# Block-sparse attention before a mixture of experts: scores of two batch elements in the two halves of the array's rows, P and V unsplit in f32

## The chip, the cores and the metric

The kernel runs on one core of a Trainium2 chip. The core has five engines that work at once, each on its own stream of instructions: TensorE (PE in the profile; its weight loads are listed as PEld), VectorE (DVE), ScalarE (ACT), GpSimd (POOL) and SyncE (SP), which here only issues transfers. 16 DMA engines move data between memory (DRAM) and the on-chip SBUF; TensorE writes its results to PSUM. A stationary matrix lies in TensorE's array, one partition of it for each row of the contraction, and the other matrix streams past it column by column. The metric is the time of one execution on the device in microseconds (us), lower is better.

## What is computed

Attention of 4 batch elements, 8 heads, 768 positions and 64 columns a head. Keys are seen in blocks of 32: every query block sees blocks 0 and 23, its own block with its two neighbours, and three blocks drawn at random; query blocks 0 and 23 see all. The output, 3072 tokens of 512 values, goes through the best of 8 experts each. Cut to what matters:

```python
scores = (1.0 / np.sqrt(D)) * np.matmul(q, k.transpose(0, 1, 3, 2))
scores = np.where(mask, scores, -1000000000.0)
scores = scores - np.max(scores, axis=-1, keepdims=True)
attn = np.exp(scores)
attn = attn / (np.sum(attn, axis=-1, keepdims=True) + 1e-09)
o = np.matmul(attn, v)
...
e_idx = np.argmax(x @ w_gate, axis=1)
for e in range(E):
    mask = e_idx == e
    h = np.maximum(x[mask] @ w1[e], 0.0)
    ye = h @ w2[e]
    out[mask] = gate_w[mask, None] * eom[mask, e, None] * ye
```

All values are f32, and the choice of the expert hangs on them, so the kernel keeps nearly f32 precision throughout.

## The kernel before

The batch elements go in two pairs (bp = 0, 1). K of a pair lies in SBUF with the 64 columns of the first element (b = 0) on partitions 0 to 63 and those of the second on 64 to 127 (`kn`). A pair has 8 dense units (query blocks 0 and 23: two elements, four groups of two heads) and 44 sparse units (11 pairs of query blocks, two elements, two groups `hg` of four heads): 104 units in all, and as many steps of the program.

A sparse unit makes these stages: **S** (`pS`), eight f32 products of 32 query columns with 256 key columns into one bank of PSUM; a maximum over the keys (`dM`, a reduction at L500 and a product with -1/8 at L501); **P** = exp (`aE`), which scales by 1/8 and subtracts the maximum on the way; **T** (`pT`), four transposes of P into PSUM; the eviction of T as two f16 tiles, 256 P rounded to f16 on ScalarE (`aH`, tile `ph`, L466) and the rest on VectorE (`dL`, tile `pl`, L473); **O** (`pO`), the product with V; a copy of O to SBUF (`aO`, tile `ob`, L537); and `fin`, `fin2`, which add the two parts of O (L446), take the reciprocal of the sum of P and multiply (L451) into the tile `x`. V too is split in f16: each head has 130 columns, 64 of 64 V rounded, a column of ones (which gives the sum of P), 64 of the rest and a zero. `ph` goes against 129 of them, `pl` against 65, so O takes 24 products. In S all 128 partitions of K and of q are used; the tiles `qz` hold the queries of one element, zeros in the other element's rows.

Keys and values come through rings. `kr` (three buffers) has the 12 blocks of K for a pair of query blocks, copied from `kn` by four engines (`gather_k`, `window_k`, `fixed`). V goes to memory (`vscr`) once, and comes back per pair of query blocks: by plain loads into `vc`, and by two indirect gathers on GpSimd's queue (`gather_v`, L423) into one of two `vt` buffers.

When x of 128 tokens is there, ScalarE casts it (`route_h`, L626) into the only `xq` buffer, GpSimd writes the rest beside it (`route_l`, L630), SP stores both to `xscr` in memory in two transfers (`store_x`, L636), a transposing load brings them back (`route_t`), and the routing's products and VectorE's routing operations follow. After the attention the experts run in slots of 128 tokens, eight pieces of weights to each; the weights are split into f16 parts by ScalarE (L891) and VectorE (L898), some by GpSimd.

Every engine issues its instructions in the order in which the program is written (`in_order`). A step of the program runs the stages of several units, each with its lag: with `LAGS = (0, 2, 3)` unit m makes S, the maximum and P in step m, T and its evictions in step m + 2, O in step m + 3, the copy of O in m + 4, `fin` and `fin2` in m + 5 and m + 6. Within a step the order is

```python
run("pT", "pS", "aH")
...
run("aE0", "dL0", "dM", "dL", "pO", "aO", "aE", "fin")
```

and loads, gathers, preparations of V and the routing are hooked to fixed steps: `at(n, f, ...)`. Dense units have `LAGD = (1, 2, 3)`, and each takes two of the four banks of scores. Units stand in the order (bp, query blocks, b, hg). In the first steps the two elements' halves of q, K and V are loaded in turn, all of b = 0 first, and from step 73 on some splits of the first experts' weights stand between the units' instructions (`AHEAD`).

## Time and profile before

| | us |
|---|---|
| three executions | 711.26, 721.58, 721.63 |
| their median | 721.58 |
| span of the profiled execution | 710.4 |

The span is the time from the first to the last instruction in the profile; the time of an execution also has what lies around it. The profiled execution's own time is not known; its span stands 0.9 us under the fastest of the three times and 11.2 us under their median.

The page and the trace's views show busy times by engine, chains of waits, groups of equal instructions and the timeline. In a group's row stand the line, the engine, the operation, result<-operands with their shapes and the count; then the busy time in us and the mean duration of one in ns; then the idle time of the engine just before them and what ended it. Durations of overlapping instructions of an engine cannot be added up; busy time counts an instant once. The page cuts the span into 40 slices, and the traffic of all its DMA engines in each was:

```profile
GB/s 223 286 259 237 236 247 304 259 224 187 156 197 276 292 270 308 192 260 53 4 294 52 154 330 157 76 230 198 227 50 137 221 61 147 211 50 60 61 264 70
```

A slice is 17.8 us. Attention is in slices 1 to 18, and the highest of those has 308 GB/s. The same row for the window from 42.5 to 309 us alone, in slices of 6.7 us, has 350 as its highest, and 331 as the highest of its last ten:

```profile
GB/s 247 221 235 282 200 140 350 217 272 273 346 254 234 241 314 140 289 284 256 66 113 168 210 246 208 155 322 271 259 257 320 268 297 278 281 331 215 196 185 317
```

### The profile page before, as it was taken

The numbers are of one execution on the slowest core, as the hardware profiler recorded it, in microseconds if no ns is written. First come the engines' busy times: TensorE is split into PE (matmuls) and PEld (weight loads), VectorE is DVE, ScalarE is ACT, GpSimd is POOL, SyncE is SP. The second block draws the span as 40 slices with busy tenths as digits, with TensorE's granted clock in tenths as the row PEclk, the third lists the DMA queues.
The fourth block names the chain that finished last, engine by engine and source line by source line (L and its number), as shares of the span: only waits on it lengthen the run. The fifth ranks groups of instructions, "written<-read, shape, count | busy, mean of one in ns | idle before, by whom it ended". The sixth has DMA issues, their size and how long they took to land.

```text
span 710.4 us, 22455 instructions
## 1 busy us (share of the span) xinstructions
PE 586.8 (83%) x8214; PEld 383.1 (54%) x8214; DVE 630.8 (89%) x999; ACT 480.3 (68%) x868; POOL 428.8 (60%) x421
## 2 busy tenths in 40 slices
PE   7878797698999888967587888888888887887886
PEld 5444454455655445546365556655555565555554
DVE  5988887788879889979579999999999999999993
ACT  2866776486688787855377676776676676676671
POOL 5556666475468887666666556556466466466461
PEclk7999999999999999987889999999999999999999
DMA  8987999897779999993082694376724724812282
GB/s 223 286 259 237 236 247 304 259 224 187 156 197 276 292 270 308 192 260 53 4 294 52 154 330 157 76 230 198 227 50 137 221 61 147 211 50 60 61 264 70
DMA packets 99054, 133.53 MB, mean 188 GB/s; under 512 B 62075, under 2 KB 69115, under 8 KB 98684
## 3 DMA queue, kind: packets, MB, share of 16 engines
q1 hardware_dynamic: 87196, 94.40, 51.7%
q0 software_dynamic: 11744, 37.64, 16.2%
q8 instruction: 67, 1.10, 0.7%
q14 instruction: 47, 0.39, 0.2%
HBM read 183.87 MB, written 20.49 MB: 288 GB/s over the span
## 4 chain that ended last, share of the span: by engine, by line
DVE 36%; DMA 22%; PE 19%; issue 13%; POOL 4%; ACT 3%; SPq 2%; POOLq 0%; ACTq 0%; DVEq 0%
DVE kr L898 17%; DMA xscr<-xq 9%; DVE ws L898 7%; PE h L909 4%; DVE hl L922 4%; PE S L494 4%; DMA vt<-vscr,vidx 3%; PE y L932 3%; PE T L459 2%; DMA kn<-in_k_dram 2%; DVE pl L473 2%; DMA out_dram<-yo,tab 2%; POOL table L757 2%; DVE mx L500 1%; DMA wide<-in_v_dram 1%
## 5 line engine op out<-in xcount | busy, mean ns | idle before, releaser
L898 DVE SCALAR_TENSOR_TENSOR kr<-r,kr 128x1024 f16<-128x1024 f32 (+1 forms) x144 | 231.4, 1655 | 9.4 <-ACT kr L891 9.3
L891 ACT ACTIVATE kr<-r 128x1024 f16<-128x1024 f32 (+1 forms) x171 | 167.0, 1031 | 11.8 <-DMA r<-in_wcat_dram 9.7
L909 PEld LDWEIGHTS <-kr 128*128 128x128 f16 x2004 | 128.6, 99 | 72.2 <-DVE kr L898 33.3
L909 PE MATMUL h<-qz,kr 128*128 128x128 f16 x1884 | 136.8, 220 | 30.5 <-DVE kr L898 28.4
L941 POOL DMA_INDIRECT out_dram<-yo,tab x28 | 30.0, 1073 | 127.3 <-ACT yo L938 121.4
L898 DVE SCALAR_TENSOR_TENSOR ws<-r,ws 128x1024 f16<-128x1024 f32 (+1 forms) x60 | 102.8, 1761 | 0.0
L932 PE MATMUL y<-kr,hh 128*128 128x512 f16 x334 | 100.3, 382 | 0.0
L506 ACT ACTIVATE P<-S,mx 128x256 f32<-128x256 f32 x176 | 75.1, 486 | 36.4 <-DVE mx L501 33.6
L494 PE MATMUL S<-kr,qz 128*32 128x256 f32 x1408 | 96.6, 393 | 0.0
L896 POOL TENSOR_TENSOR kr<-wf,kr 128x1024 f16<-128x1024 f32 x27 | 72.2, 2674 | 21.8 <-issue 10.7
L473 DVE SCALAR_TENSOR_TENSOR pl<-T,ph 128x512 f16<-128x512 f32 x88 | 60.2, 685 | 17.4 <-ACT ph L466 16.3
L500 DVE TENSOR_REDUCE mx<-S 128x2 f32<-128x512 f32 x88 | 59.5, 676 | 13.5 <-PE S L494 13.4
L932 PE MATMUL y<-kr,hl 128*128 128x512 f16 x167 | 64.0, 383 | 3.1 <-DVE hl L922 3.1
L917 ACT ACTIVATE hh<-h 128x512 f16<-128x512 f32 x56 | 33.2, 592 | 46.1 <-PE h L909 46.1
L909 PEld LDWEIGHTS <-ws 128*128 128x128 f16 x684 | 44.0, 100 | 32.4 <-DVE ws L898 18.6
L891 ACT ACTIVATE ws<-r 128x1024 f16<-128x1024 f32 (+1 forms) x60 | 58.0, 1012 | 2.1 <-PE y L932 2.1
L459 PE MATMUL T<-ident,P 128*128 128x128 f32 x352 | 59.1, 292 | 0.3 <-DVE pl0d L473 0.3
L909 PE MATMUL h<-qz,ws 128*128 128x128 f16 x612 | 45.4, 219 | 16.3 <-DVE ws L898 15.6
L466 ACT ACTIVATE ph<-T 128x512 f16<-128x512 f32 x88 | 54.1, 615 | 5.4 <-PE T L459 5.4
L853 POOL DMA_INDIRECT qz<-xscr,tab x28 | 47.9, 1710 | 11.9 <-DMA tab<-table 7.4
L938 ACT ACTIVATE yo<-y,tab 128x512 f32<-128x512 f32 x28 | 19.2, 687 | 52.9 <-PE y L932 52.9
L494 PEld LDWEIGHTS S<-kr,qz 128*32 128x32 f32 x1408 | 37.3, 110 | 31.2 <-issue 14.8
(233 smaller groups left out, 1178.3 us busy)
## 6 DMA issues: line engine op xcount, KB each, us to landing
r<-in_wcat_dram SPq DMA_DIRECT2D x240, 512.0 KB
qz<-in_q_dram SPq DMA_DIRECT2D x48, 128.0 KB
xscr<-xq SPq DMA_DIRECT2D x48, 128.0 KB
vc<-vscr SPq DMA_DIRECT2D x22, 260.0 KB
vscr<-vn SPq DMA_DIRECT2D x12, 260.0 KB
vscr<-vn SPq DMA_DIRECT2D x6, 520.0 KB
kn<-in_k_dram SPq DMA_DIRECT2D x4, 768.0 KB
vs<-in_v_dram SPq DMA_DIRECT2D x6, 512.0 KB
```

The source lines that it names most:

```text
L459: nc.tensor.transpose(pt[:, 128 * c:128 * c + 128], p[:, 128 * c:128 * c + 128], ident)
L466: nc.scalar.activation(ph[:, 0:w], pt[:, 0:w], AF.Copy, scale=SP_)
L473: nc.vector.scalar_tensor_tensor(pl[:, 0:w], pt[:, 0:w], SP_, self.ph[n][:, 0:w], op0=ALU.mult, op1=ALU.subtract)
L494: nc.tensor.matmul(s[64 * h2 + 32 * qi:64 * h2 + 32 * qi + 32, hp], t[:, 64 * j + 32 * qi:64 * j + 32 * qi + 32], g[:, 1 - qi:3:1 + qi, :, ...
L500: nc.vector.tensor_reduce(mx, self.s, axis=AX.X, op=ALU.max)
L506: nc.scalar.activation(p[:, 256 * hp:256 * hp + 256], self.s[:, hp], AF.Exp, bias=self.mx[:, hp:hp + 1], scale=EXPS)
L853: nc.gpsimd.indirect_dma_start(xgs[s], None, src, bass.IndirectOffsetOnAxis(ap=tabs[s][:, 1:2], axis=0))
L891: nc.scalar.activation(w[:, 0, r], piece(n // 8, n % 8)[:, r], AF.Copy, scale=SW)
L896: nc.gpsimd.tensor_tensor(w[:, 1], ws.pop(("f", n)), w[:, 0], op=ALU.subtract)
L898: nc.vector.scalar_tensor_tensor(w[:, 1, r], piece(n // 8, n % 8)[:, r], SW, w[:, 0, r], op0=ALU.mult, op1=ALU.subtract)
L909: nc.tensor.matmul(hps[n // 4][:, 128 * j:128 * j + 128], w[:, hl, 128 * c:128 * c + 128], x[:, c // 2, xl, c % 2], start=cnt == 0, stop=c ...
L932: nc.tensor.matmul(ys[s], a[:, m], w[:, l, 512:1024], start=n % 8 == 0 and cnt == 0, stop=n % 8 == 7 and cnt == 2)
```

## The change

Three things are done, and the order of the work follows them.

**Scores of both elements together.** `qz` is one tile per pair of query blocks with the queries of b = 0 on partitions 0 to 63 and those of b = 1 on 64 to 127; the zeros are gone. The units stand in the order (query blocks, hg, b), so that the two elements' units are neighbours, and the first of the two issues the products of both, in turn on the rows 0 to 63 and 64 to 127, into a bank of each:

```diff
         def pS(self):
+            if self.mate is None:
+                return
             bp, i, b, hg = self.k
-            t, r = qt[bp, i][b], kr[i % RK]
-            s = self.s = psS.tile([128, 2, 256], F32, tag="S", name="S" + self.name)
+            t, r = qt[bp, i], kr[i % RK]
+            both = self, self.mate
+            for u in both:
+                u.s = psS.tile([128, 2, 256], F32, tag="S", name="S" + u.name)
...
                     for qi in range(2):
-                        nc.tensor.matmul(
-                            s[64 * h2 + 32 * qi:64 * h2 + 32 * qi + 32, hp], t[:, 64 * j + 32 * qi:64 * j + 32 * qi + 32],
-                            g[:, 1 - qi:3:1 + qi, :, 32 * j:32 * j + 32], start=True, stop=True)
+                        for b, u in enumerate(both):
+                            p = slice(64 * b, 64 * b + 64)
+                            nc.tensor.matmul(
+                                u.s[64 * h2 + 32 * qi:64 * h2 + 32 * qi + 32, hp],
+                                t[p, 64 * j + 32 * qi:64 * j + 32 * qi + 32],
+                                g[p, 1 - qi:3:1 + qi, :, 32 * j:32 * j + 32], start=True, stop=True)
```

Dense units do the same, so a pair of them takes all four banks of scores at once; `LAGD` becomes (0, 2, 3). At the start q, K and then V are loaded for both elements at once:

```diff
-    load_q(0, NPAIR, (0,))
-    load_k(0, slice(0, 12), slice(0, 64))
-    load_k(0, slice(12, 24), slice(0, 64))
-    for c in range(6):
-        load_v(0, c, (0,), spare(c))
-    load_q(0, NPAIR, (1,))
-    load_k(0, slice(0, 12), slice(64, 128))
-    load_k(0, slice(12, 24), slice(64, 128))
+    load_q(0, NPAIR)
+    load_k(0, slice(0, 12))
+    load_k(0, slice(12, 24))
     for c in range(6):
-        load_v(0, c, (1,), spare(c))
+        load_v(0, c, spare(c))
```

**P and V unsplit.** A head of V has 65 f32 columns (64 and the ones) in place of 130 f16 ones, which is the same number of bytes. V's preparation is one copy per block of 128 keys (`v_in`): for the first pair on GpSimd (four) and VectorE (two), for the second all on GpSimd, where ScalarE rounded and VectorE or GpSimd subtracted before. T is evicted once, as f32, by ScalarE for units of b = 0 and by VectorE for units of b = 1 (in dense units: by ScalarE for the first half of the keys, by VectorE for the second). O takes 12 products; its copy has 65 columns a head where it had 129; the sum of the two parts (L446) is gone.

```diff
+        def evict(self, n, engine):
+            pt, w = self.t[n]
+            p = att.tile([128, 512], F32, tag="pt", name=f"pt{n}" + self.name, bufs=4)
+            if engine == "act":
+                nc.scalar.copy(p[:, 0:w], pt[:, 0:w])
+            else:
+                nc.vector.tensor_copy(p[:, 0:w], pt[:, 0:w])
+            self.pt[n] = p
...
             for hp in range(2):
-                for w, n in ((ph, 129), (pl, 65)):
-                    for h2 in range(2):
-                        col = 256 * hp + 128 + 64 * h2
+                for h2 in range(2):
+                    col = 256 * hp + 128 + 64 * h2
+                    nc.tensor.matmul(
+                        o[64 * h2:64 * h2 + 64, hp, 0:VW], w[:, col:col + 64],
+                        cv[:, b, 4 * h2 + 2 * hg + hp], start=hp == 0, stop=False)
+            for hp in range(2):
+                for h2 in range(2):
+                    for qi in range(2):
+                        col = 256 * hp + 64 * h2 + 32 * qi
                         nc.tensor.matmul(
-                            o[64 * h2:64 * h2 + 64, hp, 0:n], w[:, col:col + 64],
-                            cv[:, b, 4 * h2 + 2 * hg + hp, 0:n], start=hp == 0 and n == 129, stop=False)
...
+                            o[64 * h2 + 32 * qi:64 * h2 + 32 * qi + 32, hp, 0:VW], w[:, col:col + 32],
+                            av[:, qi, b, 4 * h2 + 2 * hg + hp], start=False, stop=hp == 1)
```

**Scale and sign.** The factor 1/8 goes into the copies of K (`eighth` in place of `one`; `fixed`, a copy on GpSimd for the first pair and three loads of 256 KB for the second, becomes two products on GpSimd each time), and a sparse unit's reduction gives the negated maximum by itself:

```diff
-            nc.vector.tensor_reduce(mx, self.s, axis=AX.X, op=ALU.max)
-            nc.vector.tensor_single_scalar(mx, mx, -EXPS, op=ALU.mult)
+            nc.vector.tensor_reduce(mx, self.s, axis=AX.X, op=ALU.max, negate=True)
```

Dense units keep their scale and sign. The experts' input buffers take three new tiles in the place of three of the six old `qz`, and `hh` and `hl` become the halves of a `pt` tile.

How the order of the engines' instructions moves is seen at the second pair's fourth pair of query blocks, on two engines. First TensorE before, from one unit's T over the start and end of the next O to the following T and S. A name has the unit's numbers (bp, i, b, hg; where there are only three, bp is left out), and the last number counts tiles; the shape is that of the result.

```order
L459 MATMUL T_1_3_0_0_5935<-ident,P_3_0_0_5829 128x128 x4
L494 MATMUL S_3_1_0_5940<-kr_182,qz_1_190 32x256 x8
L520 LDWEIGHTS ph_1_2_1_1_5866
L520 MATMUL O_2_1_1_5956<-vc_185,ph_1_2_1_1_5866 64x129
...
L528 MATMUL O_2_1_1_5956<-vt_2_5350,ph_1_2_1_1_5866 32x129
L459 MATMUL T_1_3_0_1_6006<-ident,P_3_0_1_5899 128x128 x4
L494 MATMUL S_3_1_1_6011<-kr_182,qz_1_190 32x256 x8
```

TensorE after, at the same place, from the last scores of one pair of units to the first of the next:

```order
L489 MATMUL S_3_0_0_4621<-kr_180,qz_186 32x256
L489 MATMUL S_3_1_0_4622<-kr_180,qz_186 32x256
L514 MATMUL O_2_1_0_4645<-vc_183,pt_1_2_1_0_4562 64x65 x4
L521 MATMUL O_2_1_0_4645<-vt_2_4274,pt_1_2_1_0_4562 32x65 x8
L440 MATMUL T_1_2_1_1_4684<-ident,P_2_1_1_4578 128x128 x4
L514 MATMUL O_2_0_1_4693<-vc_183,pt_1_2_0_1_4639 64x65 x4
L521 MATMUL O_2_0_1_4693<-vt_2_4274,pt_1_2_0_1_4639 32x65 x8
L440 MATMUL T_1_3_0_0_4743<-ident,P_3_0_0_4660 128x128 x4
L489 MATMUL S_3_0_1_4748<-kr_180,qz_186 32x256
L489 MATMUL S_3_1_1_4749<-kr_180,qz_186 32x256
```

Before, eight products of S stood between every T and the next O; now 16 of two units stand behind every second T, and behind the other T comes O at once.

VectorE before, at two units of the second pair (mx is the maximum, pl the rest of P, den the sum of P, ws a piece of the experts' weights):

```order
L500 TENSOR_REDUCE mx_3_1_0_5951<-S_3_1_0_5940 128x2
L501 TENSOR_SCALAR mx_3_1_0_5951<-mx_3_1_0_5951 128x2
L473 SCALAR_TENSOR_TENSOR pl_1_3_0_0_5954<-T_1_3_0_0_5935,ph_1_3_0_0_5949 128x512
L445 TENSOR_SCALAR den_2_0_1_5986<-ob_2_0_0_5827 128x4
L898 SCALAR_TENSOR_TENSOR ws_5929<-r_5353,ws_5929 128x512
L500 TENSOR_REDUCE mx_3_1_1_6022<-S_3_1_1_6011 128x2
L501 TENSOR_SCALAR mx_3_1_1_6022<-mx_3_1_1_6022 128x2
L473 SCALAR_TENSOR_TENSOR pl_1_3_0_1_6025<-T_1_3_0_1_6006,ph_1_3_0_1_6020 128x512
```

and after, at the same place:

```order
L496 TENSOR_REDUCE mx_3_0_1_4768<-S_3_0_1_4748 128x2
L896 SCALAR_TENSOR_TENSOR ws_4738<-r_4277,ws_4738 128x512
L496 TENSOR_REDUCE mx_3_1_1_4809<-S_3_1_1_4749 128x2
L449 COPY pt_1_3_1_0_4811<-T_1_3_1_0_4804 128x512
L425 TENSOR_SCALAR den_2_0_1_4830<-ob_2_0_0_4658 128x4
L426 RECIPROCAL den_2_0_1_4830<-den_2_0_1_4830 128x4
```

A reduction per unit is left, with a copy for every second one, and the split of weights now stands between the reductions of the two units of a pair. On SP the first loads of K go from four half loads, with V's between them, to two whole ones ahead of all of V.

More of the change, by code (lines that the diff above doesn't have):

```diff
@@ L63 @@
 XE = 102, 104
[L65 removed]
+VH = 17, 21, 26, 33, 37, 42
 XTB = 2
@@ L108, in tile_kernel @@
     psO = actx.enter_context(tc.tile_pool(name="psO", bufs=2, space=PSUM))
-    vscr = [dram.tile([769, 2 * 8 * VW], F16, name=f"vscr{i}") for i in range(2)]
+    vscr = [dram.tile([769, 2 * 8 * VW], F32, name=f"vscr{i}") for i in range(2)]
     xscr = dram.tile([NTOK, 2 * DM], F16, name="xscr")
@@ L322, in tile_kernel @@
     kr = [ring.tile([128, 12, 256], F32, name=f"kr{i}") for i in range(RK)]
-    vc = [ring.tile([128, 2, 8, VW], F16, name=f"vc{i}") for i in range(RV)]
-    qz = [[ring.tile([128, 512], F32, name=f"qz{n}_{b}") for b in range(2)] for n in range(RQ)]
+    vc = [ring.tile([128, 2, 8, VW], F32, name=f"vc{i}") for i in range(RV)]
+    qz = [ring.tile([128, 512], F32, name=f"qz{n}") for n in range(RQ)]
     kn, vn = {}, {}
@@ L367, in store_v, with v_in @@
+        nc.sync.dma_start(buf.rearrange("p (b j w) -> p b j w", b=2, j=8), v[bp, 128 * c:128 * c + 128])
+    def v_in(bp, c, kind):
+        vb = vn[bp][:, c].rearrange("p b j w -> p (b j) w")[:, :, 0:D]
+        vs = ld["v", bp, c].rearrange("p (n w) -> p n w", w=D)
+        if kind == "act":
+            nc.scalar.copy(vb, vs)
+        elif kind == "dve":
+            nc.vector.tensor_copy(vb, vs)
+        else:
+            nc.gpsimd.tensor_copy(vb, vs)
+    def store_v(bp, c):
         nc.sync.dma_start(
-            vscr[bp][128 * c:128 * c + 128, w * bs[0]:w * bs[-1] + w],
@@ L589, in pO @@
             for c in range(6):
-                ph, pl = self.ph[c // 3], self.pl[c // 3]
+                w = self.pt[c // 3]
                 col = 128 * (c % 3)
-                order = ((ph, 129), (pl, 65)) if c < 5 else ((pl, 65), (ph, 129))
-                for w, n in order:
-                    for h2 in range(2):
-                        j = 4 * h2 + u
-                        nc.tensor.matmul(
-                            o[64 * h2:64 * h2 + 64, 0, 0:n], w[:, col + 64 * h2:col + 64 * h2 + 64],
-                            vn[bp][:, c, b, j, 0:n], start=c == 0 and n == 129, stop=c == 5 and n == 129)
+                for h2 in range(2):
+                    nc.tensor.matmul(
+                        o[64 * h2:64 * h2 + 64, 0, 0:VW], w[:, col + 64 * h2:col + 64 * h2 + 64],
+                        vn[bp][:, c, b, 4 * h2 + u], start=c == 0, stop=c == 5)
         def aO(self):
@@ L845, in load_w @@
         nc.sync.dma_start(piece(s, j), src, cond=chg)
-    xbuf = [t for ts in qz for t in ts]
+    xbuf = qz + [ring.tile([128, 512], F32, name=f"xb{i}") for i in range(3)]
     def load_x(s):
@@ L948, in tile_kernel @@
     for bp in range(2):
-        for b in range(2):
-            for u in range(4):
+        for u in range(4):
+            for b in range(2):
                 units.append(Dense(bp, b, u))
         for i in range(NPAIR):
-            for b in range(2):
-                for hg in range(2):
+            for hg in range(2):
+                for b in range(2):
                     units.append(Sparse(bp, i, b, hg))
+    for m in range(0, len(units), 2):
+        units[m].mate = units[m + 1]
     prep_alloc(0)
@@ L996, in tile_kernel @@
     at(12, setup_index)
-    for b in range(2):
-        for c, (n, pool, early) in enumerate(VPREP[b]):
-            at(n, v_hi, 0, c, (b,), early)
-            at(n, v_lo, 0, c, (b,), pool, early)
-            at(n, store_v, 0, c, (b,))
+    for c, (n, kind) in enumerate(VPREP):
+        at(n, v_in, 0, c, kind)
+        at(n, store_v, 0, c)
     at(13, setup_rest)
```

177 lines of the change are left out of this document (72 added, 105 removed).

## The prediction

> **What bounds the kernel now.** First the busy shares, then the span by stage, then the chain of waits inside each attention stage.
>
> ```profile
> PE 586.8 (83%) x8214; PEld 383.1 (54%) x8214; DVE 630.8 (89%) x999; ACT 480.3 (68%) x868; POOL 428.8 (60%) x421
> ```
>
> The shares average over unlike stages. The windows view has one row each for the start with the first pair's dense units, its 44 sparse units, the second pair's dense units, its first 16 and last 28 sparse units, the tail of attention and routing, and the experts.
>
> ```profile
> core 0: us, PE busy (x) PEld busy (x) DVE busy (x) ACT busy (x) POOL busy (x), PEclk, DMA share, GB/s
> 0.00:42.50 42.50, 31.84 (x294) 19.68 (x294) 32.49 (x92) 21.58 (x48) 23.91 (x59) 0.88 0.92 259
> 42.50:168.60 126.10, 105.29 (x2020) 62.06 (x2019) 102.36 (x260) 86.50 (x221) 81.59 (x111) 0.96 0.92 253
> 168.60:195.50 26.90, 24.63 (x339) 14.96 (x336) 22.74 (x76) 18.11 (x47) 13.53 (x18) 0.94 0.61 134
> 195.50:234.30 38.80, 36.94 (x745) 22.17 (x744) 33.69 (x90) 31.24 (x83) 29.05 (x38) 1.00 0.89 241
> 234.30:309.00 74.70, 63.64 (x1281) 37.77 (x1280) 67.49 (x169) 57.42 (x148) 56.48 (x74) 1.00 1.06 269
> 309.00:357.00 48.00, 28.45 (x379) 22.37 (x380) 34.12 (x82) 21.99 (x38) 30.06 (x20) 0.75 0.39 76
> 357.00:710.40 353.40, 296.06 (x3169) 204.13 (x3169) 337.93 (x235) 243.50 (x288) 194.16 (x106) 0.99 0.52 152
> ```
>
> The experts hold half the span with VectorE busy 338 of 353 us, and the change leaves their arithmetic alone: it can only let them start earlier. A sparse unit takes 126.1 / 44 = 2.87, 38.8 / 16 = 2.43 and 74.7 / 28 = 2.67 us in the three sparse stages. TensorE is busy 95% of the middle one, but only 83% and 85% of the others, where the DMA share is 0.92 and 1.06. The chains of those three stages, in order, name what ends last:
>
> ```profile
> by line: DMA xscr<-xq 24.8%; DMA vt<-vscr,vidx 17.9%; PE S L494 11.8%; PE T L459 7.2%; issue 5.2%; PE O L528 3.7%; DVE mx L500 3.6%; DVE pl L473 3.5%; PE O L520 3.4%; SPq L636 2.4%; DVE mx L501 1.5%; DVE den L445 1.3%; ACT ob L537 1.2%; DVE
> by line: PE S L494 20.8%; PE T L459 10.4%; DVE pl L473 9.4%; DVE mx L500 9.4%; DVE mx L501 5.3%; PE Od L596 5.0%; PE O L520 4.1%; PE O L528 3.8%; ACT P L506 3.3%; ACT ph L466 2.8%; issue 2.7%; DVE g L697 2.3%; DVE kr L412 1.7%; PE T1d L459
> by line: DMA xscr<-xq 42.9%; issue 8.6%; PE S L494 4.6%; SPq L636 4.4%; DVE pl L473 3.4%; PE T L459 3.3%; POOL xg L853 2.6%; DVE mx L500 2.5%; SPq L376 2.5%; SPq L642 2.4%; DVE mx L501 2.2%; ACT ph L466 2.1%; ACT ob L537 2.0%; PE O L520 1.9
> ```
>
> So only the middle stage is paced by the engines that the change relieves. The other two wait on two loops of transfers: stores of x (xscr<-xq) from the one xq buffer, and the gather of V (vt) in two buffers. The timeline shows a turn of the first: a cast into xq, two stores, and the next cast, released by the landing.
>
> ```profile
> 259.48 0.62 ACT L626 CAST xq<-x 128x512 f16<-128x512 f32 x1 [1.46 <-DMA xscr<-xq]
> ...
> 262.70 1.37 SPq L636 DMA_DIRECT2D xscr<-xq  x2
> ...
> 270.96 0.62 ACT L626 CAST xq<-x 128x512 f16<-128x512 f32 x1 [2.09 <-DMA xscr<-xq]
> ```
>
> A turn is 270.96 - 259.48 = 11.5 us for four units: 2.87 each, whatever TensorE does, unless the stores land sooner.
>
> **TensorE per unit.** One steady unit on its timeline (start, duration, instruction, count):
>
> ```profile
> 207.44 1.07 PE L494 MATMUL S<-kr,qz 128*32 128x256 f32 x16
> 208.44 0.25 PE L520 MATMUL O<-vc,ph 128*64 128x129 f16 x2
> 208.52 0.20 PE L520 MATMUL O<-vc,pl 128*64 128x65 f16 x2
> ...
> 208.87 0.23 PE L528 MATMUL O<-vt,ph 128*32 128x129 f16 x4
> 209.03 0.66 PE L459 MATMUL T<-ident,P 128*128 128x128 f32 x4
> 209.61 0.42 PE L494 MATMUL S<-kr,qz 128*32 128x256 f32 x4
> ```
>
> S takes 208.44 - 207.44 = 1.00, O 0.59, T 0.58: together 2.17.
>
> - Scores. Eight f32 products stand as 16 rows in four column strips, four deep: 0.25 us for 256 columns, 0.98 ns a column and row. The change puts 16 products for two units there, half of them on rows 0-63 and half on 64-127. If the halves run at once, the pair costs 1.00, or 0.50 a unit; if they take turns, 1.00 a unit. No row here shows two row halves at once. I take overlap, since the column strips do overlap, and keep 1.00 as the other end.
> - P times V. Eight f16 products of 64 columns and 16 of 32 become four and eight in f32, each two rows of 65 columns. Per strip: 2 + 2 products, two rows each, 8 x 65 x 0.98 = 0.51 us streaming. Before, the strip streamed 4 x (129 + 65) = 776 columns; the f16 price follows from products of 512 and 128 columns,
>
> ```profile
> L932 PE MATMUL y<-kr,hh 128*128 128x512 f16 x334 | 100.3, 382 | 0.0
> L909 PE MATMUL h<-qz,kr 128*128 128x128 f16 x1884 | 136.8, 220 | 30.5 <-DVE kr L898 28.4
> ```
>
>  (382 - 220) / 384 = 0.42 ns a column, 0.33 us; so 0.59 - 0.33 = 0.26 was gaps. With all or half of these O becomes 0.77 or 0.64: I take 0.70 (ends 0.51 and 0.90).
> - T is unchanged. New unit: 0.50 + 0.70 + 0.58 = 1.78, a saving of 0.39 (18%).
>
> **The other engines per unit.** ScalarE, VectorE and GpSimd:
>
> ```profile
> L466 ACT ACTIVATE ph<-T 128x512 f16<-128x512 f32 x88 | 54.1, 615 | 5.4 <-PE T L459 5.4
> L473 DVE SCALAR_TENSOR_TENSOR pl<-T,ph 128x512 f16<-128x512 f32 x88 | 60.2, 685 | 17.4 <-ACT ph L466 16.3
> L500 DVE TENSOR_REDUCE mx<-S 128x2 f32<-128x512 f32 x88 | 59.5, 676 | 13.5 <-PE S L494 13.4
> L501 DVE TENSOR_SCALAR mx<-mx 128x2 f32<-128x2 f32 x88 | 29.9, 339 | 3.0
> L446 POOL TENSOR_TENSOR ob<-ob 128x256 f32<-128x256 f32 x41 | 26.7, 650 | 0.0
> L405 POOL TENSOR_TENSOR kr<-kn,one 128x256 f32<-128x256 f32 x66 | 46.0, 697 | 3.7 <-DVE mxd L574 3.2
> L382 POOL COPY kr<-kn 128x512 f32<-128x512 f32 x3 | 1.9, 626 | 0.0
> ```
>
> Each T was evicted twice (615 on ScalarE, then 685 on VectorE); now once, in turn. ScalarE loses 0.31 a unit. VectorE loses 0.685 + 0.339 (the negation goes into the reduction, which stays at 676) and gains half an f32 copy, at 685 at most 0.34: net -0.68. In the middle stage ScalarE was busy 31.24 / 16 = 1.95 a unit and VectorE 2.11; they go to 1.64 and 1.43, under TensorE's 1.78. The exp without a scale and K's copies with one keep their durations: zero, as the copies already multiply (L405 by one). GpSimd loses 27 us of sums of hi and lo. It gains six copies of V (1024 columns; twice the 512-column copy's 626 is 1.25 each, 7.5 in all) and 12 - 3 fixed copies of K at 697, less than 7: about 15, in stages where it is 65% busy. A gather of vt queued behind one of them starts up to 1.25 later; the other end, nothing. The eviction's halves bring one new wait: odd units' O now waits on VectorE alone, behind the expert weights' splits there; before, every O did, through pl. Loads: one 128-partition q instead of two halves takes an issue per pair off SP's queue; V's store and gather move the same bytes (65 f32 for 130 f16).
>
> **Sum by stage.**
> - Start. Its end is tied to V's way to the gather, and first scores wait for K:
>
> ```profile
> 3.15 9.76 DMA wide<-in_v_dram
> 12.92 13.17 DMA kn<-in_k_dram
> 32.42 4.72 DMA vscr<-vn
> 43.98 8.78 DMA vt<-vscr,vidx
> 8.62 1.08 PE L564 MATMUL S0d<-kn,qz 64*64 64x384 f32 x4 [2.71 <-DMA kn<-in_k_dram]
> ```
>
>  Two rounds of half loads end in K at 26.1 and V's store at 32.4. Now K comes whole, then V; q, K and V are 6.6 MB, 25 us at the row's 259 GB/s, and one copy and store follow: about 28 instead of 32. I take -5; ends -9, and +3 if first scores wait for all of K's first half and the dense units run late.
> - Sparse, first pair. If TensorE paced it: 44 x 0.39 = -17. By the chain's shares: PE S, T and O hold 26% of 126 us, of which 18% is 5.9; the negation 1.9; half of pl 2.2: -10. I take -13. Ends: 0 if the loops hold, and -22 if the same bytes moved at the best slice of the page, 308 GB/s, in place of 253.
> - Dense, second pair. A dense pair now takes all four score banks at once, so the next pair's scores wait for the exps: fewer products, a new wait. -2 (-5 to +2).
> - Next 16 units: TensorE-paced, 16 x 0.39 = -6 (0 to -8).
> - Last 28 units: PE shares 10% of 75 us by 18%, negation 1.6, half of pl 1.3: -4; TensorE-paced would be -11. I take -6; ends 0, and -14 at the best slice again (269 to 331).
> - Tail and experts: 0 (5 either way); they start earlier.
>
> Sum: -5 - 13 - 2 - 6 - 6 = -32. The profiled execution's span is 710.4, 0.9 under the fastest run and 11.2 under the median 721.6; its new span would be 678.4. Against the median: 721.6 - 32 = 689.6.
>
> A rule against the full gain: the Trainium skill, TensorEngine Tiling (Array Packing), section "PSUM Bottleneck", says that tiling speeds up TensorE and not the emptying of PSUM, which may then bound. By it the dense pair, whose four banks wait for reductions and exps, would gain 0 rather than 2, and the sum would be -30. The same page, "Key Properties", says that different tiles run matmuls in parallel; by it scores cost 0.50 a unit. No run yet shows either for row halves.
>
> **Rivals.**
> - Loops shrink too. Fewer stalls let SP issue the stores sooner, and the two loops follow TensorE: -5 - 22 - 2 - 8 - 14 = -51, about 671. For: steps pace the issue of the stores. Against: the DMA share is already 0.92 and 1.06. Chance 0.14.
> - Loops hold all. Only start, dense and the middle stage gain: -5 - 2 - 6 = -13, 708.6. For: the 42.9% of the last chain. Against: PE, pl and mx stand on the chains too. Chance 0.18.
> - Row halves take turns. Scores of a pair take 2.00, so a unit is 1.00 + 0.70 + 0.58 = 2.28, 0.11 over now; 88 x 0.11 = +10 gives 731, and with O at 0.90, +27 gives 749. It decides from 1.78 a pair on. For: no row of overlap. Against: the strips overlap. Chance 0.07.
> - The forecast (676 to 707): 0.58. Unnamed slowdowns: 0.03. A lower granted clock is in these: the tail's row has 0.75 at 59% busy, but the first pair's stage would be 88 / 113 = 78% busy, near its 83% with 0.96.
>
> **Numbers.** 2% is 14.4 us (707.2 to 736), about what a measurement of this kernel can tell from no change. Faster: 0.58 + 0.14 + 0.02 of the second rival = 0.74; slower 0.06 (the third with its worse O, and unnamed); same 0.20. The range runs from 662, below the first rival for a longer bound of its 51, to 710, past the second: some 0.2 is left out, mostly above.
>
> **What would show it.** Right: scores of a pair in 1.0 us; O near 0.7; about 1.8 to 2.0 a unit on TensorE in the middle stage; xscr<-xq still heading the last stage's chain with a turn near 11 us; the first sparse scores near 37; experts still 353 us. Wrong: a pair's scores at 2 us; stores landing in 5 us; the dense stage over 29 us; or the experts' stage longer, as its own splits would then hold what attention gave.

## The result and the profile after

| | before | after |
|---|---|---|
| executions (us) | 711.26, 715.08, 721.58, 721.63 | 683.72, 692.33, 692.40, 693.10 |
| median | 718.33 | 692.37 |
| span of the profiled execution | 710.4 | 691.3 |

The changed kernel takes 0.9634 of the time before, 95% interval 0.9534 to 0.9735: faster, by 26 us between the medians. The forecast was 689.6, in a range of 662 to 710. Some executions take over 1.5% longer than the fastest of their kernel; the ratios here and below leave them out, the medians do not. The profiled execution of the changed kernel was its slowest (693.10 for a span of 691.3); that of the kernel before, whose time is not known, has a span 0.9 us under its fastest time. The spans therefore differ by 19 only.

The windows view of the changed kernel, cut at the same places of the program (start, first pair's sparse units, second pair's dense units, its first 16 and last 28 sparse units, tail, experts):

```profile
core 0: us, PE busy (x) PEld busy (x) DVE busy (x) ACT busy (x) POOL busy (x), PEclk, DMA share, GB/s
0.00:35.00 35.00, 26.82 (x296) 17.70 (x296) 20.57 (x79) 12.26 (x28) 16.93 (x51) 0.85 0.90 331
35.00:146.50 111.50, 93.82 (x2020) 61.21 (x2019) 73.01 (x183) 67.52 (x188) 72.88 (x95) 0.97 0.98 281
146.50:174.70 28.20, 23.58 (x335) 15.68 (x333) 21.30 (x65) 14.08 (x37) 13.52 (x18) 0.88 0.58 116
174.70:212.40 37.70, 33.95 (x747) 22.89 (x746) 27.31 (x67) 26.64 (x76) 26.99 (x33) 1.00 0.81 228
212.40:290.50 78.10, 63.92 (x1260) 40.74 (x1263) 46.55 (x127) 48.13 (x133) 50.10 (x60) 0.89 1.00 259
290.50:338.00 47.50, 28.58 (x414) 21.93 (x405) 31.75 (x77) 21.01 (x37) 29.30 (x18) 0.82 0.38 81
338.00:691.30 353.30, 295.33 (x3165) 202.97 (x3163) 337.53 (x235) 243.83 (x288) 195.49 (x106) 0.99 0.52 152
```

By stage the change gave -7.5, -14.6, +1.3, -1.1, +3.4, -0.5 and -0.1 us: 19.1 less in all. Each is the difference of two single executions. How far a stage moves from one execution to the next is seen in two runs below that leave the first pair's sparse stage as it was: it takes 119.1 us in before_start, where the kernel before has 126.1, and 108.0 in after_pre, where the changed kernel has 111.5. VectorE's busy time in the three sparse stages fell from 204 to 147 us and ScalarE's from 175 to 142, and still the last 28 units did not get shorter. What the reader is to see is the last column but one: the DMA engines are busy 0.98 and 1.00 of the two long stages. (The share adds up the times of packets, so it can pass 1, as the 1.06 before did.) The chains of the three sparse stages, in order (issue is time for which the profile shows no wait; SPq and POOLq are the sequencers of SP and GpSimd):

```profile
by line: DMA xscr<-xq 41.6%; issue 14.1%; DMA xT<-xscr 6.1%; PE S L489 4.9%; POOL x L430 4.5%; POOL kr L385 4.2%; POOLq L376 3.6%; PE T L440 2.8%; SPq L634 2.3%; POOL vn L349 1.9%; PE O L514 1.4%; PE O L521 1.3%; POOL vt L403 1.3%; SPq L640
by line: DMA vt<-vscr,vidx 25.8%; DMA xscr<-xq 22.2%; PE T L440 13.8%; PE S L489 12.6%; PE Od L594 6.8%; PE O L521 6.1%; PE O L514 5.1%; issue 4.4%; POOL xq L628 3.1%; POOL vt L403 1.9%; ACT xq L624 1.7%; POOL x L430 1.5%; PE T0d L440 1.3%;
by line: DMA xscr<-xq 47.3%; issue 14.3%; DMA tab<-table 10.5%; DMA table<-vals,place 7.0%; POOL x L430 4.6%; SPq L640 4.3%; POOL vt L403 4.3%; POOL kr L385 2.6%; SPq L634 2.5%; POOL xg L851 2.5%; SPq L822 2.3%; POOL xq L628 2.3%; POOLq L37
```

Transfers now end last in the middle stage too, where TensorE did before. TensorE itself did become quicker. Its timeline at a pair's scores, and at a sparse unit:

```profile
179.10 1.09 PE L489 MATMUL S<-kr,qz 64*32 64x256 f32 x32
180.12 0.57 PE L594 MATMUL Od<-vn,pt0d 128*64 128x65 f32 x12
...
201.31 0.64 PE L440 MATMUL T<-ident,P 128*128 128x128 f32 x4
201.88 0.45 PE L514 MATMUL O<-vc,pt 128*64 128x65 f32 x8
202.26 0.44 PE L521 MATMUL O<-vt,pt 128*32 128x65 f32 x16
202.63 0.66 PE L440 MATMUL T<-ident,P 128*128 128x128 f32 x4
```

The 16 products of two units (32 records, two for each product) take 180.12 - 179.10 = 1.02 us, where the eight of one took 1.00: the row halves run at once. O takes 202.63 - 201.88 = 0.75. With T at 0.58 a unit costs 0.51 + 0.75 + 0.58 = 1.84, against 2.17 before. The groups of the other engines:

```profile
L496 DVE TENSOR_REDUCE mx<-S 128x2 f32<-128x512 f32 x88 | 59.7, 682 | 44.1 <-PE S L489 34.0 <-PE O L514 10.0
L449 DVE COPY pt<-T 128x512 f32<-128x512 f32 x44 | 29.9, 680 | 5.7 <-PE T L440 2.2 <-remote 1.7 <-PE O L521 1.7
L349 POOL COPY vn<-vs 128x1024 f32<-128x1024 f32 x6 | 6.7, 1113 | 0.0
L447 ACT COPY pt<-T 128x512 f32<-128x512 f32 x44 | 25.8, 587 | 30.6 <-PE T L440 25.6 <-remote 3.5 <-PE S L489 1.3
```

The negated reduction stays at its price (682 against 676 ns), the f32 eviction costs VectorE 680 and ScalarE 587, and V's copies 1.11 us each. VectorE's reductions now wait 44 us for TensorE, where they waited 13.5.

### The profile page after: what moved, and what is told of

It is laid out like the page before. It is cut to its first block, busy times and chain, and to the rows that moved or that the text cites. A ratio compares the mean times of both kernels' runs of the same rounds, so it can differ in the third digit from the quotient of the medians.

```text
span 691.3 us, 22003 instructions
## 1 busy us (share of the span) xinstructions
PE 566.0 (82%) x8214; PEld 383.1 (55%) x8214; DVE 558.0 (81%) x829; ACT 433.5 (63%) x784; POOL 405.2 (59%) x379
## 4 chain that ended last, share of the span: by engine, by line
DVE 34%; DMA 23%; issue 16%; PE 14%; POOL 7%; SPq 2%; ACT 2%; POOLq 1%; another core or an unknown queue 0%; DVEq 0%; ACTq 0%
DVE kr L896 19%; DMA xscr<-xq 12%; DVE ws L896 7%; DVE hh L923 4%; PE h L907 3%; PE y L933 2%; POOL table L755 2%; DMA kn<-in_k_dram 2%; DMA tab<-table 2%; DMA out_dram<-yo,tab 2%; PE S L489 1%; DMA vt<-vscr,vidx 1%; POOL x L430 1%; DMA r<-in_wcat_dram 1%; PE T L440 1%
## 5 line engine op out<-in xcount | busy, mean ns | idle before, releaser
L889 ACT ACTIVATE kr<-r 128x1024 f16<-128x1024 f32 (+1 forms) x171 | 167.0, 1031 | 11.6 <-DMA r<-in_wcat_dram 9.5
L933 PE MATMUL y<-kr,hh 128*128 128x512 f16 x501 | 138.3, 381 | 3.3 <-DVE hh L923 2.9
L907 PE MATMUL h<-xb,kr 128*128 128x128 f16 x1344 | 98.1, 220 | 22.5 <-DVE kr L896 21.3
L933 PEld LDWEIGHTS <-hh 128*128 128x128 f16 x672 | 57.1, 99 | 42.8 <-DVE hh L923 15.0
L628 POOL TENSOR_TENSOR xq<-x,xq 128x512 f16<-128x512 f32 x24 | 29.2, 1216 | 62.9 <-ACT xq L624 60.9
L489 PE MATMUL S<-kr,qz 64*32 64x256 f32 x1408 | 62.2, 405 | 3.8 <-issue 3.1
L918 ACT ACTIVATE hh<-h 128x512 f16<-128x512 f32 x56 | 33.2, 592 | 47.5 <-PE h L907 46.6
L440 PE MATMUL T<-ident,P 128*128 128x128 f32 x352 | 59.5, 293 | 0.0
L403 POOL DMA_INDIRECT vt<-vscr,vidx x44 | 44.8, 1018 | 24.6 <-PE O L521 11.2
L521 PE MATMUL O<-vt,pt 128*32 128x65 f32 x1408 | 44.1, 233 | 15.1 <-DMA vt<-vscr,vidx 12.2
L885 POOL TENSOR_TENSOR wf<-r,sw 128x1024 f32<-128x1024 f32 x27 | 52.6, 1947 | 4.5 <-DMA r<-in_wcat_dram 3.9
L514 PE MATMUL O<-vc,pt 128*64 128x65 f32 x704 | 42.2, 239 | 15.7 <-ACT ob L530 11.6
L514 PEld LDWEIGHTS O<-vc,pt 128*64 128x64 f32 x704 | 29.3, 141 | 44.6 <-ACT ob L530 21.2
```

Source lines behind the costliest of these rows:

```text
L403: nc.gpsimd.indirect_dma_start(t[:, s].rearrange("p b j w -> p (b j w)"), None, vscr[bp], bass.IndirectOffsetOnAxis(ap=vidx[:, i, s:s + 1] ...
L440: nc.tensor.transpose(pt[:, 128 * c:128 * c + 128], p[:, 128 * c:128 * c + 128], ident)
L489: nc.tensor.matmul(u.s[64 * h2 + 32 * qi:64 * h2 + 32 * qi + 32, hp], t[p, 64 * j + 32 * qi:64 * j + 32 * qi + 32], g[p, 1 - qi:3:1 + qi, ...
L514: nc.tensor.matmul(o[64 * h2:64 * h2 + 64, hp, 0:VW], w[:, col:col + 64], cv[:, b, 4 * h2 + 2 * hg + hp], start=hp == 0, stop=False)
L885: nc.gpsimd.tensor_tensor(wf, piece(n // 8, n % 8), sw128.to_broadcast([128, 1024]), op=ALU.mult)
L889: nc.scalar.activation(w[:, 0, r], piece(n // 8, n % 8)[:, r], AF.Copy, scale=SW)
```

## The experiments

Each was compared with the kernel before on its own chip; the ratio is of times, with its 95% interval. For the changed kernel itself it is 0.963 (0.953 to 0.974). The profiles of after_xq2, after_pre and after_neg have spans 10, 10 and 9 us above the medians of their times, so a stage that is longer there proves nothing. A difference between two ratios, of runs on different chips, is given with both intervals taken together (as independent).

| run | median us | before us | ratio |
|---|---|---|---|
| after_xq2 | 697.3 | 717.9 | 0.974 (0.967 to 0.981) |
| after_own | 759.7 | 717.9 | 1.062 (1.053 to 1.071) |
| after_block, one time | 699.4 | 717.9 | |
| before_pair | 736.2 | 717.9 | 1.027 (1.018 to 1.035) |
| after_turn | 681.2 | 720.5 | 0.952 (0.942 to 0.962) |
| after_zero | 704.6 | 720.5 | 0.981 (0.972 to 0.989) |
| after_pre | 680.1 | 720.5 | 0.949 (0.941 to 0.957) |
| after_turn_pre | 678.9 | 713.2 | 0.957 (0.947 to 0.967) |
| after_turn_pre_xq2 | 676.4 | 713.2 | 0.950 (0.934 to 0.966) |
| after_neg | 692.1 | 713.2 | 0.974 (0.963 to 0.985) |
| before_start | 712.1 | 713.2 | 1.002 (0.996 to 1.008) |
| zero_turn_pre_xq2 | 709.8 | 718.6 | 0.989 (0.980 to 0.997) |

### Is it the one xq buffer?

```diff
-            xq = rt.tile([128, 2, 2, 256], F16, tag="xq", name=f"xq{tt}", bufs=1)
+            xq = rt.tile([128, 2, 2, 256], F16, tag="xq", name=f"xq{tt}", bufs=2)
```

> The changed kernel with two xq buffers in place of one, nothing else. Theory A (one xq buffer holds the two long sparse stages: a cast waits for the landing of the stores before it, and ScalarE's and GpSimd's queues stand behind it): no cast waits for a landing any more, the last 28 units go from 78 us to 62-68, the first pair's 44 from 111.5 to 97-104, total 18 to 28 us under the changed kernel. Rival B (the transfers' bandwidth is the bound, the wait only shows it): the stages shrink by less than 3 us each, total within 5 us of the changed kernel. Rival C (the gather of vt in its two buffers takes over): half of A, 8 to 14 us.

Not faster: the ratio is 1.0% above the changed kernel's, give or take 1.2. A and C are excluded. B fits, at the edge of its 5 us (697.3 against 692.4): neither long stage shrank, with 117.3 and 81.4 us in a profile 10 us above the median. The waits of the first pair's sparse stage (who waits for whom: us in total, times, longest):

```profile
ACT pt L447 <- PE T L440: 22.8, 10, 6.2
...
PEld O L521 <- DMA vt<-vscr,vidx: 8.5, 3, 5.5
PEld L664 <- DMA xT<-xscr: 8.1, 4, 2.7
...
PE lp L664 <- DMA xT<-xscr: 7.4, 4, 2.6
```

No cast waits for a landing any more. In its place TensorE waits, with its whole queue, for the transposing load of x (the product lp) and for the gather of vt, and ScalarE waits for TensorE. The wait moved one station down the same trip; the buffer did not hold the stage. In the last 28 units the landing of the stores still has 39.8% of the chain (47.3% with one buffer), with the transposing load behind it at 12.2%.

### Do the row halves overlap, and what does pairing give?

The first run takes the mate away, the second only changes the order of a pair's products:

```diff
-            if self.mate is None:
-                return
...
-            both = self, self.mate
+            both = (self,)
...
```

> The changed kernel, but every unit issues its own eight scores' products (on its 64 rows) in its own step: no two row halves at once. If row halves overlap in the changed kernel, S of a unit costs 1.0 us here and 0.64 there. Theory A (TensorE paces only the 16 units in the middle): those 16 units are 4 to 6 us longer, the other sparse stages within 4 us, the dense stage of the second pair 1 to 2 us shorter since no four banks are taken at once; total 2 to 9 us over the changed kernel. Rival (TensorE paces all sparse stages): 0.36 x 88 = 30 us over it.

```diff
-            for hp in range(2):
-                for h2 in range(2):
-                    j = 4 * h2 + 2 * hg + hp
-                    for qi in range(2):
-                        for b, u in enumerate(both):
+            for b, u in enumerate(both):
+                for hp in range(2):
+                    for h2 in range(2):
+                        j = 4 * h2 + 2 * hg + hp
+                        for qi in range(2):
```

> The changed kernel with the 16 products of a sparse pair in another order: eight of the first row half, then eight of the second, in place of taking turns. If the halves run at once only when neighbours in the queue lie on different halves, S of a pair takes 2.0 us in place of 1.28; if TensorE looks further ahead than eight products, it stays at 1.28. If the halves never ran at once in the changed kernel, nothing changes.

In after_block the timeline has a pair's scores at full clock and the O behind them:

```profile
190.61 1.13 PE L489 MATMUL S<-kr,qz 64*32 64x256 f32 x32
191.67 0.45 PE L514 MATMUL O<-vc,pt 128*64 128x65 f32 x8
```

191.67 - 190.61 = 1.06 us: the halves still run at once when eight products of one half stand in the queue ahead of the other's. (The 1.28 in the expectations was the first pair of the changed kernel's middle stage, at 174.72 us; the next took 1.02, and the granted clock was 1.00 at both. Why the first took longer is not shown.) In after_own a unit's scores take 1.0 us, as expected, but the total is 67 us over the changed kernel, more than either theory. The page's row of the granted clock in after_own, by slices of 18.9 us:

```profile
PEclk9999555555559999998888999999999999999999
```

and the window of its low stretch, in the windows view:

```profile
83.30:200.80 117.50, 117.50 (x1303) 64.51 (x1302) 44.02 (x116) 43.65 (x118) 44.25 (x56) 0.50 0.66 173
```

For 117 us TensorE was busy without a pause at half its clock. The clock fell in a stall, of 5.0 us up to 80.8 us, and came back at 229 us, 150 us later, in the second pair's dense units. All four executions have a low mean clock (0.86 to 0.88; the changed kernel's have 0.95 to 0.96), so it is no chance of one profile. So a second experiment gave every unit its own scores with all 128 rows in use, the other element's being zeros, as in the kernel before. It is the unsplit P and V without the pairing:

```diff
-            t, r = qt[bp, i], kr[i % RK]
+            t, r = qt[bp, i][b], kr[i % RK]
...
-                            p = slice(64 * b, 64 * b + 64)
+                            p = slice(0, 128)
...
```

> The changed kernel, but every unit issues its own eight scores' products on all 128 rows, with zeros in the other element's rows (as the kernel before): P and V unsplit alone, with scale, sign and start of the changed kernel. TensorE's unit is 1.0 + 0.75 + 0.59 = 2.33 us, as in the run with 64 rows and no pairs (759.7). Theory K (with products on 64 of the 128 rows only, the granted clock stays at a half once it fell; with all rows in use it comes back within some 7 us): no stretch of 0.5 over 15 us in the sparse stages, first pair's sparse stage 108-120 in place of 163 us, total 695 to 712. Rival (the stretch at half clock came from TensorE having no idle time, whatever the rows): about 755.

Theory K held: 704.6, 55 us under after_own with the same products per unit. Its windows of the first pair's sparse stage and of the last 28 units:

```profile
37.10:163.90 126.80, 112.41 (x2022) 68.81 (x2021) 71.27 (x178) 67.36 (x188) 69.18 (x88) 0.93 0.95 248
228.30:307.80 79.50, 67.61 (x1275) 41.01 (x1276) 51.63 (x125) 47.54 (x133) 49.49 (x58) 1.00 1.06 255
```

The clock is back at 0.93 and 1.00: it fell in stalls here too (of 4.8 us up to 126.8 us, for one), and was at 1.00 again 7 to 10 us after it fell. The first stage is 127 us, over the 108 to 120 expected. Against the kernel before, unsplit P and V with their scale, sign and start give 1.9%; pairing then gives the rest, 704.6 to 692.4 (1.7%, give or take 1.3). By stage, in one execution of each, the first pair's sparse units take 126.1 us before, 126.8 without pairs and 111.5 with them: nearly all of that stage's gain stands with the pairing, although the DMA share was 0.95 without it. The start has its gain without pairs already (42.5, 37.1 and 35.0 us).

The other order, pairing first, was tried on the kernel before. It needs the changed kernel's loads at the start, and V's preparation for both elements in the first two steps:

```diff
+            both = self, self.mate
+            for u in both:
+                u.s = psS.tile([128, 2, 256], F32, tag="S", name="S" + u.name)
...
-    ((4, False, False), (4, True, False), (4, False, False), (5, True, False), (5, False, False), (5, False, False)))
+    ((1, False, False), (1, True, False), (1, False, False), (2, True, False), (2, False, False), (2, False, False)))
```

> The kernel before with the scores of both elements in pairs alone (with it the order of units, the loads of q, K and V for both elements at the start, the lag of dense units); P and V stay split, scale and sign too. Theory A (the xq loop holds the long stages): the gain is at the start (5 to 8 us) and in the 16 middle units (0.36 x 16 = 6), and next to nothing in the other sparse stages; 8 to 16 us under the kernel before. Rival (TensorE paces): 0.36 x 88 + 6 = 38 us under it, more than the whole change gave.

It is 2.7% slower than the kernel before; both theories had it faster. Its start and first pair's sparse stage:

```profile
0.00:52.30 52.30, 30.30 (x294) 18.93 (x294) 31.88 (x92) 20.90 (x46) 24.81 (x59) 0.74 0.73 256
52.30:179.90 127.60, 97.46 (x2020) 60.34 (x2019) 110.17 (x259) 87.26 (x222) 80.34 (x105) 0.89 0.83 232
```

Ten us are lost at the start, whose chain has V's split there (VectorE 16.6%, ScalarE 7.0%). Beyond it the sparse stage did not shrink: VectorE, which keeps both evictions' second half and the sign, is the busiest engine (110 us), and TensorE, with less to do, ran at 0.89 of its clock. Nor did the middle 16 units, which TensorE paced before: 45.2 us against 38.8, with a clock of 0.86 and chains headed by the stores of x and by VectorE; the second pair's dense units take 4.3 us more. How much of the loss is V's place in the first steps, how much the order of units and how much the clock, this run does not separate.

### Is it the time of the DMA engines?

Two edits take DMA time out of the long stages without touching a buffer. In the first x is turned (transposed) by TensorE and not by a transposing load, into the same xT buffers:

```diff
...
-            if tt < NT - 2:
-                at(t0 + r2, route_t, tt)
-            else:
-                at(t0 + r2, turn, bp, i, tt)
+            at(t0 + r2, turn, bp, i, tt)
```

> The changed kernel with x of every tile of tokens turned by TensorE (four transposes, a copy on ScalarE and a subtraction on VectorE, as the last two tiles do it) in place of the transposing load from xscr; the stores to xscr stay. Theory D (in the two long sparse stages the 16 DMA engines are busy for the whole stage: 109.8 of 111.5 us and 78.2 of 78.1; transposing loads are 21 and 17 us of it): the stages go to 92-100 and 62-68 us, total 20 to 30 us under the changed kernel. Theory A' (what holds is the trip x - xscr - xT - product, however busy the DMA engines are): the same direction, 10 to 25 us. Rival T (TensorE and the clock): longer by 0.6 us of TensorE for four units, 26 x 0.6 = 14 us over it.

In the second, weights of the first experts are loaded in the dense stage, where the DMA share was 0.58:

```diff
-        at(per + 14 + 2 * j, prefetch_w, j)
+        at(per + 2 + j if j < 6 else per + 2 + 2 * j, prefetch_w, j)
```

> The changed kernel with the first twelve weight loads (512 KB each) one dense stage earlier: six in the dense stage of the second pair, five in its first 16 sparse units, one in the last 28 (before: none, five, seven). Theory D (DMA engines' time is the bound of the last 28 units): that stage loses 6 x 1.7 = 10 us of DMA time and goes from 78 to 66-71 us, the dense stage (16.5 of 28.2 us of DMA time) stays within 2 us; total 6 to 11 us under the changed kernel. Theory A (waiting for landed stores, not for the DMA engines' time): within 3 us of it.

With x turned, the two long stages are

```profile
34.60:136.10 101.50, 93.35 (x2056) 64.11 (x2055) 81.96 (x195) 72.16 (x197) 71.86 (x95) 0.98 0.91 290
201.60:266.50 64.90, 56.01 (x1262) 38.81 (x1263) 52.30 (x127) 47.86 (x130) 44.70 (x52) 0.97 0.89 255
```

101.5 and 64.9 us in place of 111.5 and 78.1, although TensorE, ScalarE and VectorE do more. The first is 1.5 us over what D gave it, the second within. Some 1.5 us of the second difference is the cut: in the profiles of after_zero, after_pre, after_turn and the last two kernels below the last window ends at the start of the last scores, in the changed kernel 1.5 us behind it (the last scores start at 289.0 us, which gives 76.6 for the stage). The total fell by 11 us only, not 20 to 30 (by the ratios 1.1%, give or take 1.4). Tail and experts took 42.3 + 364.8 = 407.1 us, where they took 47.5 + 353.3 = 400.8: 1.5 of these 6 us are the cut, 3.8 lie between the last scores and the first output (53.8 us against 50.0), and 1.0 behind it.

After_pre is 12 us under the changed kernel, just past what D gave it, with not an instruction fewer: the same loads at another time. By the ratios it is 1.4%, give or take 1.3, the only one of the runs with less DMA work in the long stages whose total stands clear of the changed kernel. Its profile, of an execution 12 us over the median, has the middle and the last stage at

```profile
169.80:207.60 37.80, 33.14 (x749) 22.59 (x748) 28.23 (x67) 25.84 (x77) 26.98 (x34) 0.95 0.99 253
207.60:279.40 71.80, 56.32 (x1238) 36.63 (x1239) 47.59 (x120) 44.76 (x125) 47.87 (x57) 0.90 0.93 203
```

The last stage is 4.8 us shorter than 76.6, just short of the 66 to 71 that D gave it. The middle one has a DMA share of 0.99 and is no longer than with 0.81: a share near one does not by itself show that the DMA engines hold a stage. Both runs point the same way, and that a mere move of loads does it speaks against the trip of x as the only holder (theory A). A rival stays open: the moved loads also no longer stand between the stores of x in SP's order, and no run separates that from the DMA engines' time.

Both together, and then with two xq buffers:

> The changed kernel with both edits that take DMA time out of the last 28 units: x turned by TensorE, and the first weights loaded a stage earlier. Theory D: there the DMA engines would be busy 47 of 65 us, so they no longer hold the stage and other waits do (stores of x before the next cast, GpSimd's queue); the second edit adds less than alone: 2 to 7 us under the run with x turned (681.2), so 674 to 679. Rival (both gains add up): 669 or less.

> The same with two xq buffers. Two buffers made the changed kernel 5 us slower while the DMA engines were full. Theory D: now that they have idle time the cast's wait for landed stores (19% and 26% of the chains of the second pair's sparse stages with x turned) is what holds, and the second buffer takes it away: 4 to 12 us under the run with one buffer. Rival (the buffer never held anything): within 3 us of it.

678.9 is in D's range: the second edit adds little to the first, and the ratios (0.957 and 0.952) cannot tell them apart. The second buffer took 2.6 us more off the median, less than D's 4 to 12 and within the intervals; whether it holds anything there stays open. The last kernel's long stages:

```profile
36.50:136.80 100.30, 91.28 (x2056) 62.94 (x2055) 83.36 (x195) 71.95 (x197) 69.99 (x90) 1.00 0.90 293
...
208.00:267.50 59.50, 56.48 (x1264) 38.59 (x1263) 53.24 (x127) 47.90 (x130) 44.00 (x52) 0.97 0.83 223
```

In the last 28 units TensorE is now busy 56.5 of 59.5 us, so it holds that stage. Part of the gain is paid back: the second pair's dense units and first 16 sparse units take 30.8 and 40.4 us, where the changed kernel has 28.2 and 37.7. If the DMA engines held the last stage before, pairing must be worth more here than it was in the change. The last run takes the pairing away again, with zeros as in after_zero:

> The unpaired kernel (every unit its own scores on 128 rows with zeros, 704.6 us) with the three edits of the best run: x turned by TensorE, first weights loaded earlier, two xq buffers. It tells what pairing is worth where the DMA engines have idle time. TensorE's sparse unit is 2.33 us here against 1.85 in pairs. Theory D (pairing gave 12 us in the changed kernel, 704.6 to 692.4, because the DMA engines held the long stages): here the sparse stages are paced by TensorE, 88 x 0.48 = 42 us of it at most, so this kernel is 25 to 42 us over the paired one (676.4): 701 to 718, hardly less than the unpaired kernel without the edits. Rival (pairing is worth some 12 us in any surrounding, the edits their 16): about 688.

```profile
39.40:157.70 118.30, 112.63 (x2057) 70.59 (x2055) 81.34 (x189) 72.08 (x197) 68.82 (x88) 1.00 0.84 246
...
231.50:306.30 74.80, 70.42 (x1298) 43.97 (x1300) 59.98 (x131) 52.45 (x142) 49.25 (x60) 1.00 0.80 210
```

709.8, within D's 701 to 718: pairing is worth 33 us between the medians here (3.8% by the ratios, give or take 1.8), against 12 in the change (1.7%, give or take 1.3). The two intervals overlap; it is the stages that tell more, in one execution of each kernel. In the last 28 units pairing is worth 74.8 - 59.5 = 15.3 us here, against 79.5 - 76.6 = 2.9 in the change, as D has it. In the first pair's sparse stage it is worth 18.0 here and 15.3 in the change, though the DMA share was 0.98 there: D alone does not explain that stage, in which TensorE without pairs was busy 112.4 of 126.8 us. TensorE is busy 95% and 94% of the long stages, with DMA shares of 0.84 and 0.80. Without pairing the same three edits bring nothing to the total (704.6 and 709.8): the long stages are 8.5 and 4.7 us shorter, the second pair's dense and middle units 5.0 and 4.4 longer.

### Sign and start

```diff
-            nc.vector.tensor_reduce(mx, self.s, axis=AX.X, op=ALU.max, negate=True)
+            nc.vector.tensor_reduce(mx, self.s, axis=AX.X, op=ALU.max)
+            nc.vector.tensor_single_scalar(mx, mx, -1.0, op=ALU.mult)
```

> The changed kernel with the sign of a sparse unit's maximum in an instruction of its own again (88 of 339 ns on VectorE, 30 us of its busy time). Theory D (VectorE has idle time in every attention stage: 73 of 111.5, 27 of 37.7, 47 of 78 us busy): within 4 us of the changed kernel. Rival (the chain reduction, sign, exp is on the path): up to 0.34 x 88 = 30 us over it.

692.1 against 692.4 for the changed kernel; the ratios, 0.974 and 0.963, differ by 1.1%, give or take 1.5. So of the 30 us of instructions the total shows none for certain, some 8 by the ratios, and 18 at most; the rival's full 30 are excluded, a part of them is not.

```diff
-    load_q(0, NPAIR, (0,))
-    load_k(0, slice(0, 12), slice(0, 64))
-    load_k(0, slice(12, 24), slice(0, 64))
...
+    load_q(0, NPAIR)
+    load_k(0, slice(0, 12))
+    load_k(0, slice(12, 24))
```

> The kernel before with the start's loads of the changed one alone (q, K in two loads, then V in six, all for both elements). If the half loads on 64 partitions held the start, the first sparse scores come at 36 to 39 in place of 42.5 us, and the total falls by 3 to 7 us. Rival (V's preparation and the dense units hold it): 41 to 44, no change.

No change in the total, and the first sparse scores came at 46.5 us, later than the 42.5 before:

```profile
0.00:46.50 46.50, 37.81 (x294) 22.04 (x294) 33.83 (x94) 21.79 (x48) 25.37 (x59) 0.71 0.70 245
```

So the whole loads alone bring no gain. Whether they would at an equal clock is not shown: the start has a granted clock of 0.71 here against 0.88 before, and its DMA share fell from 0.92 to 0.70. In after_zero, which has the changed kernel's loads and its unsplit V but no pairs, the sparse scores start at 37.1 (clock 1.00). That leaves V's preparation, six copies where 24 operations on three engines wrote it, and the dense units' shorter stages as the likely gain; no run has one of these alone.

## Why the prediction was right

The sum was -32, the medians give -26, and the direction and the range held. That 692.4 lies so near 689.6 is in part luck: the forecast counted from the median of three times, 721.6, and with a fourth time that median is 718.3. What the prediction named as the sign of its mechanism came: the stores of x head the last stage's chain, with turns of 11.6, 11.8 and 10.7 us (stores at 207.69, 219.25, 231.04 and 241.72 us in the chain). Step by step:

- **TensorE per unit.** Forecast 0.50 + 0.70 + 0.58 = 1.78, measured 0.51 + 0.75 + 0.58 = 1.84. The rival in which row halves take turns is excluded by 1.02 us for 16 products, and 1.06 in the other order. The Trainium skill, TensorEngine Tiling (Array Packing), "Key Properties", says that tiles run in parallel: the trace agrees. O came out near the upper of its two values: the gaps stayed, as the number of records did (24 a unit before and after); that this is why is a reading.
- **Other engines.** The reduction kept its time (682 ns), the f32 eviction cost 680 and 587, V's copies 1.11 us against an estimate of 1.25. The sign was priced at 1.9 and 1.6 us in the long stages; after_neg allows anything from nothing to 18.
- **Start, -5.** Measured -7.5, but the reason given, whole loads, brought no gain alone. (The 32.4 of its working is where a store of V begins in that chain; it lands at 37.1.)
- **First pair's sparse units, -13.** Measured -14.6, or anything from -7.6 to -18.1 with the executions of before_start and after_pre, so the size was right within what one execution tells. The reason was half so. The loop through the one xq buffer was taken for what holds the stage, and the DMA engines' fullness for a sign of it. With a second xq buffer the same stage waits elsewhere, and with x turned it takes 101.5: that speaks for the transfers' time and against the buffer.
- **Second pair's dense units, -2.** Measured +1.3, with a clock of 0.88 in this execution; 25.8 us, or -1, in after_block with a clock of 1.00. By the rule of the Trainium skill weighed there (TensorEngine Tiling (Array Packing), "PSUM Bottleneck") the gain would be 0: the two runs lie on either side of it and do not decide it.
- **Middle 16 units, -6, and last 28 units, -6.** Measured -1.1 and +3.4. These are the terms that were mis-sized. The middle stage was held to be TensorE's; relieved of it, TensorE met the gather of vt and the stores, which now have 25.8% and 22.2% of its chain. In the last stage the bound of the transfers was known (a DMA share of 1.06 before), and the term should have been its lower end, 0: 20.1 MB took 74.7 us before, and 20.3 MB took 78.1 in the changed kernel, with a share of 1.00. The best slices, 308 and 331 GB/s, were no measure for a whole stage: no run's long sparse stage passed 293.
- **The rival "loops hold all"** (708.6) gave the first pair's stage nothing, where it gained 14.6 us with the DMA share going from 0.92 to 0.98, and was right in the last one.

## What to carry to other kernels

When a stage's DMA share is near one, a wait for a landing can be a symptom: here a buffer more only moved the wait, and less work for the DMA engines, or the same loads at another time, went with a shorter stage. The share alone does not prove it (0.99 cost the middle stage of after_pre nothing), so move the load and look. What a faster engine is worth can be measured by undoing it in both surroundings (in the last 28 units 2.9 us with full DMA engines, 15.3 with idle time). Where an engine is relieved, its stage's next bound must be priced from the trace before the whole gain is booked.

## What the runs showed of the hardware that was not expected

The granted clock of TensorE does not follow its busy time alone. With scores on 64 of the 128 rows, one unit at a time, the clock fell to 0.50 during a stall of 5.0 us and stayed there for 150 us, of which the window above has 117 without a gap in TensorE's record (busy 117.50 of 117.50); with zeros in the other 64 rows, and the same number of products, it was back at 1.00 some 7 us after it fell in a stall of 4.8 us, and the first pair's sparse stage has 0.93 on the mean and takes 127 us in place of 164. In pairs, both halves are in use and the clock comes back too (0.97). The Trainium skill, TensorE: Matmul & The Clock Gate, "What's actually happening", says that recent activity of TensorE opens the gate, after some 3.4 us of it; this stretch does not agree if activity is time busy. That rows in use count is a reading of these three runs; the zeros were changed together with the rows, and no run separates them. Nor is it the whole account: the clock came back at 229 us in dense units, whose scores stand on 64 rows too (in products of 64 query columns with 384 key columns). Later in the same kernel, with the same sparse products, the clock was 1.00 in the second pair's first 16 sparse units (41.2 us): scores on half the rows were enough to keep the gate open, and in the first pair's sparse units did not open it again.
